# One more pair of feed-forward steps in joined form, in four blocks of a fused RWKV-6 and feed-forward kernel

## The chip, the cores and the metric

The kernel runs on one core of a Trainium2 chip. The metric is the device time of one execution in microseconds (us). All data are float32 in memory; a float32 matmul is issued as two instructions, so counts of matmul instructions in the profile are twice the number of products.

The engines are named as in the profile: PE (TensorE matmuls), PEld (its weight loads), DVE (VectorE), ACT (ScalarE), POOL (GpSimd) and SP (SyncE, which issues most DMAs).

## The reference

```python
batch, n_heads, seq, head_dim = (4, 8, 768, 48)
n_tokens, d_model, d_ff = (3072, 384, 2048)
...
for t in range(S):                       # RWKV-6: a recurrence over the tokens
    kt, vt, rt, wt = (k[:, :, t], v[:, :, t], r[:, :, t], w[:, :, t])
    cur = np.einsum('bhd,bhe->bhde', u[None] * kt, vt)
    y[:, :, t] = np.einsum('bhd,bhde->bhe', rt, state + cur)
    state = wt[:, :, :, None] * state + np.einsum('bhd,bhe->bhde', kt, vt)
...
x = y.transpose(0, 2, 1, 3).reshape(B * S, H * D)
h = x @ w_in
g = h - np.tanh(h)
return (g @ w_out).astype(np.float32)
```

## The kernel before

**Blocks and steps.** The 3072 tokens are worked in 8 blocks of 384 (`NB`), two for each of the 4 sequences. A block's attention output lies in three tiles `xT` of 128 features by 384 tokens. The feed-forward part of a block runs over 16 steps `f`, each for 128 of the 2048 hidden units. The main loop (L1340) runs over the blocks `i` and in each over the steps; `now` is 16 i + f. While the steps of block i run, the attention of block i+1 (`later`) is prepared between them: its operations are put by `plan(i)` (L1145) to certain steps, and DMAs for i+1 and i+2 (`after`) too. For blocks 3 to 6 the plan puts `times_behind` to steps 0 and 1 and `times_before` and `held` to step 3 (all on DVE), the score product `earlier` (PE, the method `gram`, L497) to step 4, the splits, DMA transposes and joins that turn the keys to steps 3 to 9 (the turned keys are collected in the tile `ks`), `update` (PE, L578, the first reader of v) to step 10 and `results` (PE, L772, then ACT copies into `xT` and `late`) to step 12.

**A single step.** `first` (L884) makes h of 128 hidden units by 384 tokens with 3 products (6 instructions, L886) into the PSUM tile `hp`, and ACT scales it (L891). `slight` (L966) then makes g: on ACT the square s of h (L978), a second square qa (L979) and a check (`over`, L983), on DVE two products (L894), the second of which writes g. DVE's two products are not issued with their step but in the next one, as `rest`.

**The second matrix product.** For two steps together (a pair q = f // 2), `form_g` (L1012) makes sums and differences of the six 128x128 pieces of g on DVE, and `Fewer` (L1077) multiplies them with forms of `w_out` in 15 products instead of 18. Six of them are issued by `add` at step 2q+3 and six at step 2q+4; the list `due` holds what is to come, and `add_due` issues it. With the last pair of a block, `add` also evicts the PSUM banks by ACT (`scaled`, L1103); this falls to steps 1 and 2 of the next block. Three products for each pair, the side products, come later (`others`, in part in steps 0 and 1 of the next block, into one of the two PSUM tiles `att`), and `others_summed` (L1118, DVE) reads them.

**A joined pair.** `Twos` (L897) makes h of two steps at once. `weight_forms` (L917) makes five combinations s1 to s5 of the pieces of `w_in`, `token_forms` (L926) four combinations t1 to t4 of the halves of `xT[0]` and `xT[1]`, each 192 tokens wide. `begin` (L934) then issues 11 products of 192 columns (22 instructions, L950) instead of 6 of 384, into both tiles `att`; ACT copies one of the sums (L951), and four DVE additions (L960) give h of both steps, held in the tiles `pre` and `w`. In the kernel before, the pairs 0 to 6 of block 7 and the pair 7 of block 6 (`BEFORE`) are joined; there, no attention work of a next block needs those tiles any more. All forms of `w_in` are made in block 6.

**The order.** PE, DVE, ACT and SP are scheduled by hand (`tc.manual_schedule`): each engine carries its instructions out in the order in which the code issues them. In each step the order is: `first` or `begin`, `slight`'s ACT part, the DVE list `ops`, the phases of the next block, the loads, and what is due. The list `ops` is put together from `rest` (the products of the step before), `formed` and `forming` (forms of g; the second stem from two steps before), `carried`, `behind`, and `spare` (the next block's DVE work); `between` takes two lists in turn. In the even step of a joined pair, `add_due` is called before `slight`. A load may be held back behind the step's scaling instruction, `made` (L1497).

Of the kernel before, what the change touches and what calls it, by code (L numbers as in the profile page):

```python
# [37 lines left out]
F32 = mybir.dt.float32  # L38
# [27 lines left out]
DM = H * D  # L66
FF = 2048
KC = DM // P
NF = FF // P
N = B * S  # L70
BANK = 512
HB = NB // 2
# [46 lines left out]
        ("add", (0, 4, 0), (11, 2, 11)), ("sub", (14, 14, 1)))  # L119
PLACES = ((8, 10, 0), (2, 5, 13), (11, 7, 14))  # L120
TWOS = range(7)
BEFORE = NF // 2 - 1


SLIGHT = 2.0 ** -6
# [4 lines left out]
def kernel(  # L130
# [144 lines left out]
    class Kept:  # L275
# [3 lines left out]
        def __init__(self, pool):  # L279
            self.both, self.n = [pool.tile([P, 2, BANK], F32, name=f"att{j}", tag=f"att{j}") for j in range(2)], 0  # L280
# [42 lines left out]
    class Block:  # L323
# [86 lines left out]

        def begin(self):
            self.xT = [xpool.tile([P, NB], F32, name=f"xT{i}", tag=f"xT{i}") for i in range(KC)]
            self.late = inp.tile([P, NB], F32, name="late", tag="late")
            return self.xT

        def before(self, p0, n):
# [318 lines left out]
        def result_out(self, pairs, copy=None):  # L735

            copies = []
            for p in reversed(pairs):
                n = p // 2
# [153 lines left out]
    def product(out, in0, scalar, in1, op0):  # L893
        return lambda: nc.vector.scalar_tensor_tensor(out=out, in0=in0, scalar=scalar, in1=in1,  # L894
                                                      op0=op0, op1=ALU.mult)

    class Twos:  # L897

        def __init__(self):
            def spare(name):
                return inp.tile([P, 2 * HALF], F32, name=name, tag=name)

            n = NF // 2 * P
            k, r, post = spare("k"), spare("r"), spare("post")
            self.forms = [t[:, 0:n].rearrange("p (j c) -> p j c", c=P) for t in (k, r, post)]
            self.turned = [t[:, n + a * HB:n + (a + 1) * HB] for t in (k, r) for a in range(2)]
            self.to = None

        def more(self):
            n = NF // 2 * P
            ks = work.tile([P, NPAIR * NCP * P], F32, name="ks", tag="ks", bufs=1)
            v_sb = inp.tile([P, NCP * DM], F32, name="v_sb", tag="v_sb")
            self.forms += [t[:, 0:n].rearrange("p (j c) -> p j c", c=P) for t in (ks, v_sb)]

        def weight_forms(self, late):  # L917

            at = w_in_sb.rearrange("p (j two) k c -> p j two k c", two=2)
            (a11, a12, a13), (a21, a22, a23) = ([at[:, :, i, k] for k in range(KC)] for i in range(2))  # L920
            s1, s2, s3, s4, s5 = self.forms if late else self.forms + [None] * 2
            return [lambda op=op, of=of: nc.vector.tensor_tensor(out=of[0], in0=of[1], in1=of[2], op=OPS[op])
                    for op, *of in (("add", s1, a21, a22), ("sub", s2, s1, a11), ("sub", s3, a11, a21),
                                    ("sub", s4, a12, s2), ("sub", s5, a13, a23))[2 if late else 0:5 if late else 2]]

        def token_forms(self, xs):  # L926
# [3 lines left out]
            t1, t2, t3, t4 = self.turned  # L930
            return [lambda of=of: nc.vector.tensor_tensor(out=of[0], in0=of[1], in1=of[2], op=ALU.subtract)
                    for of in ((t1, b12, b11), (t3, b22, b12), (t2, b22, t1), (t4, b21, t2))]

        def begin(self, ps, j):  # L934

            if self.to is None:
                self.to = [inp.tile([P, 2 * HALF], F32, name=name, tag=name)[:, 0:8 * HB].rearrange(
                    "p (n t) -> p n t", t=HB) for name in ("pre", "w")]
            h = self.to[j % 2]
            e0, e1 = ps.both[(ps.n + 1) % 2], ps.both[ps.n % 2]  # L940
            (a11, a12, a13), (_, a22, a23) = ([w_in_sb[:, 2 * j + i, k] for k in range(KC)] for i in range(2))
            s1, s2, s3, s4, s5 = (t[:, j] for t in self.forms)
            t1, t2, t3, t4 = self.turned
            (b11, _), (b21, b22), (b31, b32) = self.first, self.second, self.third
            for to, *of in ((e0[:, 1, 0:HB], (a11, b11)), (e0[:, 0, 0:HB], (a12, b21), (a13, b31)),
                            (e0[:, 0, HB:NB], (s2, t2)), (e1[:, 0, 0:HB], (s3, t3)),
                            (e1[:, 0, HB:NB], (s1, t1), (a23, b32)), (e1[:, 1, 0:HB], (s4, b22), (s5, b32)),
                            (e1[:, 1, HB:NB], (a22, t4), (a23, b31))):
                for n, (lhs, rhs) in enumerate(of):
                    nc.tensor.matmul(to, lhsT=lhs, rhs=rhs, start=n == 0, stop=n + 1 == len(of))  # L950
# [9 lines left out]
            return [lambda of=of: nc.vector.tensor_tensor(out=of[0], in0=of[1], in1=of[2], op=ALU.add)  # L960
                    for of in ((h[:, 0:5:4], twice(h[:, 7]), both(e0[:, 0, 0:NB])),
                               (h[:, 5:7], twice(h[:, 4]), both(e1[:, 0, 0:NB])),
                               (h[:, 1], h[:, 6], e1[:, 1, 0:HB]),
                               (h[:, 2:4], twice(h[:, 5]), e1[:, 1::-1, HB:NB]))]
# [180 lines left out]
    def plan(i):  # L1145
# [15 lines left out]
        else:  # L1161
# [178 lines left out]
    for i, blk in enumerate(blocks):  # L1340
# [9 lines left out]
        for f in range(NF):  # L1350
# [19 lines left out]
            if not joined:  # L1370
                g, ahead_of_h, square, later_ops = slight(h, now, i, f)
            elif f % 2:
                g, ahead_of_h, square, later_ops = slight(twos.h[1], now, i, f, 1.0 / UPSCALE, over)
                for op in over:
                    op()
            else:
                ahead_of_h, square = [], []
# [8 lines left out]
                              if of and not name.startswith("bound")]  # L1386
            if i:
                spare += [lambda n=n: form_w(n, 4 if f < 12 else 6, 2) for n in formed_w.get(f, ())]
            if i == blocks_n - 2:
                if f == 10:  # L1390
                    twos = Twos()
                    spare += twos.weight_forms(False)
                elif f == 13:
                    twos.more()
# [202 lines left out]
```

## Time and profile before

| | |
|---|---|
| time, median of 3 runs | 543.28 us (542.43 to 544.0) |
| profiled execution | 543.27 us, span 541.4 us |
| mean granted TensorE clock | 0.995 of full speed |
| PE busy | 531.2 us (98%) |
| DVE busy | 481.2 us (89%) |
| ACT busy | 396.7 us (73%) |
| block 3, steps 0 to 15 | 216.56 to 280.45 us of the span |
| block 6, steps 0 to 15 | 408.31 to 471.8 us of the span |

The span runs from the first to the last instruction; the time around it is not in the rows. In the rows of a timeline the first number is the start in us from the span's start, the second the length of the group in us, then the engine, the line, the operation, the tiles out<-in, the shape and the count; in brackets stands the engine's idle time before it and what ended it. Matmuls are pipelined, so the length of a group ends later than the next one starts; the distance between two starts is what a group costs. In the rows of groups by shape the numbers behind the bar are busy time in us and the mean of one in ns.

### The profile page before, as it was taken

The numbers are of one execution on the slowest core, as the hardware profiler recorded it, in microseconds if no ns is written. First come the engines' busy times: TensorE is split into PE (matmuls) and PEld (weight loads), VectorE is DVE, ScalarE is ACT, GpSimd is POOL, SyncE is SP. The second block draws the span as 40 slices with busy tenths as digits, with TensorE's granted clock in tenths as the row PEclk, the third lists the DMA queues.
The fourth block names the chain that finished last, engine by engine and source line by source line (L and its number), as shares of the span: only waits on it lengthen the run. The fifth ranks groups of instructions, "written<-read, shape, count | busy, mean of one in ns | idle before, by whom it ended". The sixth has DMA issues, their size and how long they took to land.

```text
span 541.4 us, 15092 instructions
## 1 busy us (share of the span) xinstructions
PE 531.2 (98%) x5780; PEld 415.0 (77%) x5780; DVE 481.2 (89%) x992; ACT 396.7 (73%) x800; POOL 9.3 (2%) x57
## 2 busy tenths in 40 slices
PE   7899999999999999999999999999999999999996
PEld 5756666677887778777877787777877777899994
DVE  7899999999989989799897889979897899979985
ACT  5899996888668876688676887588865986546461
POOL 1100000000000000000000000000000000000001
PEclk9899999999999999999999999999999999999999
DMA  7698632261402632154212532137222320100011
GB/s 276 230 404 333 240 101 96 90 144 60 123 18 80 159 108 69 45 129 138 61 56 61 131 120 65 51 90 161 62 89 68 78 72 17 42 1 0 12 35 47
DMA packets 53048, 56.35 MB, mean 104 GB/s; under 512 B 21488, under 2 KB 50928, under 8 KB 52976
## 3 DMA queue, kind: packets, MB, share of 16 engines
q1 hardware_dynamic: 52592, 55.18, 33.9%
q8 instruction: 49, 0.80, 0.6%
q14 instruction: 23, 0.19, 0.1%
q10 hardware_dynamic: 288, 0.10, 0.1%
q0 software_dynamic: 96, 0.07, 0.1%
HBM read 44.73 MB, written 4.72 MB: 91 GB/s over the span
## 4 chain that ended last, share of the span: by engine, by line
PE 94%; DVE 3%; DMA 1%; issue 1%; SPq 0%; DVEq 0%
PE hp L886 39%; PE acc L1091 27%; PE att L1091 6%; PE acc L1042 5%; PE att L950 5%; PE att L772 4%; PE att L497 2%; PE att L578 1%; PE acc L1069 1%; PE att L886 1%; DMA r<-in_rT 1%; PE acc L886 1%; DVE pre L420 1%; PE hp L1091 0%; PE att L682 0%
## 5 line engine op out<-in xcount | busy, mean ns | idle before, releaser
L886 PE MATMUL hp<-xT,w_sb 128*128 128x384 f32 x642 | 225.6, 488 | 0.5 <-DVE w_sb L271 0.5
L886 PEld LDWEIGHTS hp<-xT,w_sb 128*128 128x128 f32 x642 | 114.8, 190 | 61.2 <-issue 0.6
L1091 PE MATMUL acc<-forms,g 128*128 128x128 f32 x972 | 135.7, 276 | 0.0
L1091 PEld LDWEIGHTS acc<-forms,g 128*128 128x128 f32 x972 | 124.2, 192 | 8.8
L1012 DVE TENSOR_TENSOR g<-g 128x256 f32<-128x256 f32 x270 | 106.5, 420 | 6.4 <-PE acc L1091 5.7
L891 ACT ACTIVATE h<-hp 128x384 f32<-128x384 f32 x107 | 52.6, 491 | 77.6 <-PE hp L886 77.5
L894 DVE SCALAR_TENSOR_TENSOR h<-h,s 128x384 f32<-128x384 f32 x112 | 61.7, 551 | 26.1 <-ACT s L978 25.8
L979 ACT ACTIVATE qa<-s,shift 128x384 f32<-128x384 f32 x113 | 69.6, 616 | 3.7
L983 ACT ACTIVATE junk<-s,shift 128x384 bf16<-128x384 f32 x113 | 67.9, 600 | 0.3
L1091 PE MATMUL acc<-w_sb,g 128*128 128x128 f32 x324 | 54.0, 276 | 0.0
L1091 PEld LDWEIGHTS acc<-w_sb,g 128*128 128x128 f32 x324 | 47.3, 192 | 8.7 <-ACT sums L1059 0.3
L894 DVE SCALAR_TENSOR_TENSOR g<-qa,h 128x384 f32<-128x384 f32 x96 | 52.9, 551 | 0.7
L978 ACT ACTIVATE s<-h 128x384 f32<-128x384 f32 x97 | 50.7, 523 | 3.0
L1126 DVE TENSOR_TENSOR sums<-sums 128x256 f32<-128x256 f32 x84 | 33.4, 410 | 1.2 <-ACT sums L1103 1.0
L1042 PE MATMUL acc<-w_sb,sums 128*128 128x384 f32 x96 | 33.7, 487 | 0.0
L1091 PE MATMUL att<-w_sb,g 128*128 128x128 f32 x200 | 33.4, 275 | 0.0
L267 ACT ACTIVATE up<-raw 128x768 f16<-128x768 f32 (+1 forms) x32 | 33.4, 1080 | 0.0
L1091 PEld LDWEIGHTS att<-w_sb,g 128*128 128x128 f32 x200 | 29.0, 192 | 4.2
L1042 PEld LDWEIGHTS acc<-w_sb,sums 128*128 128x128 f32 x96 | 18.0, 190 | 12.3 <-DVE sums L894 0.3
L420 DVE TENSOR_TENSOR_SCAN pre<-w,start 128x780 f32<-128x780 f32 x14 | 25.0, 1783 | 0.8
L432 DVE TENSOR_TENSOR_SCAN post<-w,seed 128x780 f32<-128x780 f32 x14 | 24.9, 1776 | 0.0
L983 ACT ACTIVATION_READ_ACCUMULATOR junk<-s,shift 128x1 f32 x113 | 21.1, 187 | 0.0
(156 smaller groups left out, 653.5 us busy)
## 6 DMA issues: line engine op xcount, KB each, us to landing
raw<-in_weights SPq DMA_DIRECT2D x16, 768.0 KB, 6.6
w<-in_wT SPq DMA_DIRECT2D x7, 780.0 KB, 4.6
k<-in_kT SPq DMA_DIRECT2D x7, 768.0 KB, 4.5
r<-in_rT SPq DMA_DIRECT2D x7, 768.0 KB, 4.6
v_sb<-in_v SPq DMA_DIRECT2D x8, 576.0 KB, 4.0
k<-in_tokens SPq DMA_DIRECT2D x7, 576.0 KB, 4.9
r<-in_tokens SPq DMA_DIRECT2D x7, 576.0 KB, 4.8
out_y<-sums SPq DMA_DIRECT2D x18, 128.0 KB, 1.8
```

Source lines behind the costliest of these rows:

```text
L267: return lambda: nc.scalar.activation(out=to, in_=of, func=AF.Copy, scale=scale, bias=bias)
L420: return nc.vector.tensor_tensor_scan(out=self.tile("pre")[:, cols], data0=self.tile("w")[:, cols], data1=start[:, 0:n * NCH * LP], initia ...
L886: nc.tensor.matmul(hp, lhsT=w_in_sb[:, f, kc, :], rhs=xT[kc], start=(kc == KC - 1), stop=(kc == 0))
L891: return h, nc.scalar.activation(out=h, in_=hp, func=AF.Copy, scale=1.0 / UPSCALE)
L894: return lambda: nc.vector.scalar_tensor_tensor(out=out, in0=in0, scalar=scalar, in1=in1, op0=op0, op1=ALU.mult)
L978: nc.scalar.activation(out=s, in_=h, func=AF.Square, scale=scale)
L979: nc.scalar.activation(out=qa, in_=s, func=AF.Square, bias=shift[:, 4:5])
L983: nc.scalar.activation(out=junk[:, 0:NB], in_=s, func=AF.Relu, bias=shift[:, 5:6], accum_out=excess[:, at:at + 1])
L1012: return lambda: nc.vector.tensor_tensor(out=G[:, to:to + 2], in0=two(G, g_at(q, a0), g_at(q, a1)), in1=two(G, g_at(q, b0), g_at(q, b1)), ...
L1042: nc.tensor.matmul(acc, lhsT=g[:, j * P:(j + 1) * P], rhs=w_out_sb[:, f, :], start=(f == self.first), stop=(f == NF - 1))
L1091: nc.tensor.matmul(to, lhsT=G[:, g_at(q, a), :], rhs=rhs, start=start, stop=stop, skip_group_check=True)
L1126: ops.append(lambda op=op, at=at: nc.vector.tensor_tensor(out=at[0], in0=at[1], in1=at[2], op=OPS[op]))
```

## The change

Pair 1 (steps 2 and 3) of blocks 3 to 6 is joined too. A second object of `Twos`, `beside`, holds the forms for this one pair. It is made anew in each of the four blocks. The weight forms are made in step 0 of the block and lie, with the first two token forms, in the tile of v (`v_sb`), which is idle then; the token forms are made in step 1, the last two in the tile `late`. The h of the pair goes to the tile `ks`. The load of v for the next block moves from step 1 to step 5. In step 3 of these blocks, and in step 15 of block 6, the DVE list is `forming[:1] + rest + formed + spare`, where it was `forming[:1]` and then `rest + formed` and `spare` in turn.

For the last two blocks, the token forms of block 6 (made in step 13) lie in the unused ends of `post` and `ks` instead of those of `k` and `r`. Those of block 7 keep `k` and `r`; they are made in step 14 of block 6 instead of step 15.

```diff
-BEFORE = NF // 2 - 1
+JOINED = {3: (1,), 4: (1,), 5: (1,), 6: (1, NF // 2 - 1), 7: TWOS}
...
+            if i in JOINED:
+                loads = {3: ["tokens k"], 4: ["tokens r"], 5: ["v"], 7: ["w"], 9: ["k"], 11: ["r"]}
...
-            joined = f // 2 in TWOS if not later else i == blocks_n - 2 and f // 2 == BEFORE
+            joined = f // 2 in JOINED.get(i, ())
+            near = later and f < 4
...
-                outs = twos.begin(ps_a, f // 2)
+                by = beside if near else twos
+                outs = by.begin(ps_a, f // 2)
...
+            if later and i in JOINED and f < 2:
+                if not f:
+                    beside, v_left, late_left = (Twos(1, 1), spare_tile("v_sb", NCP * DM), spare_tile("late", NB))
+                    for x in range(5):
+                        beside.form(x, v_left, x * P)
+                    beside.results(spare_tile("ks", NPAIR * NCP * P, work))
+                    spare += beside.weight_forms(0, 2, 1, 4, 3)
+                else:
+                    spare += beside.token_forms(here, beside.halves((v_left, 5 * P), (late_left, 0)))
             if i == blocks_n - 2:
                 if f == 10:
-                    twos = Twos()
-                    spare += twos.weight_forms(False)
+                    twos = Twos(0, NF // 2)
...
+                    spare += twos.weight_forms(0, 1)
                 elif f == 13:
...
-                    spare = twos.token_forms(here) + twos.weight_forms(True) + spare
-                elif f == 15:
-                    spare += twos.token_forms(xT)
+                    spare = (twos.token_forms(here, twos.halves((post_left, left), (ks_left, left))) +
+                             twos.weight_forms(2, 3, 4) + spare)
+                    twos.results(*(spare_tile(name) for name in ("pre", "w")))
+                elif f == 14:
+                    spare += twos.token_forms(xT, twos.halves((k_left, left), (r_left, left)))
...
-            elif joined and (later or f < 2 * LAST):
+            elif joined and later:
+                ops, carried = forming[:1] + rest + formed + spare, forming[1:]
+            elif joined and f < 2 * LAST:
                 ops, carried = forming[:1] + between(rest + formed, spare), forming[1:]
...
-                g, ahead_of_h, square, later_ops = slight(twos.h[0], now, i, f, 1.0 / UPSCALE, over)
+                g, ahead_of_h, square, later_ops = slight(by.h[0], now, i, f, 1.0 / UPSCALE, over)
```

The lines left out pass the tiles to `Twos` from outside (`form`, `halves`, `results`) where it took them itself, and create the tile `late` at its first use.

More of the change, by code (lines that the diff above doesn't have):

```diff
@@ L412, in begin @@
             self.xT = [xpool.tile([P, NB], F32, name=f"xT{i}", tag=f"xT{i}") for i in range(KC)]
-            self.late = inp.tile([P, NB], F32, name="late", tag="late")
+            self.late = None
             return self.xT
@@ L738, in result_out @@
             for p in reversed(pairs):
+                if self.late is None:
+                    self.late = inp.tile([P, NB], F32, name="late", tag="late")
                 n = p // 2
@@ L895, in product, with spare_tile @@
                                                       op0=op0, op1=ALU.mult)
+    def spare_tile(name, width=2 * HALF, pool=inp):
+        return pool.tile([P, width], F32, name=name, tag=name, bufs=1)
     class Twos:
[L901 to L919, printed above, removed]
+        def __init__(self, base, n):
+            self.base, self.n = base, n
+            self.forms, self.to = [None] * 5, []
@@ new lines, in form, with halves, results, weight_forms @@
+        def form(self, x, t, at=0):
+            self.forms[x] = t[:, at:at + self.n * P].rearrange("p (j c) -> p j c", c=P)
+        def halves(self, *tiles):
+            return [t[:, at + a * HB:at + (a + 1) * HB] for t, at in tiles for a in range(2)]
+        def results(self, *tiles):
+            self.to = [t[:, 0:8 * HB].rearrange("p (n t) -> p n t", t=HB) for t in tiles]
+        def weight_forms(self, *which):
+            at = w_in_sb[:, 2 * self.base:2 * (self.base + self.n)]
+            at = at.rearrange("p (j two) k c -> p j two k c", two=2)
@@ L920, in weight_forms @@
             (a11, a12, a13), (a21, a22, a23) = ([at[:, :, i, k] for k in range(KC)] for i in range(2))
-            s1, s2, s3, s4, s5 = self.forms if late else self.forms + [None] * 2
+            s1, s2, s3, s4, s5 = self.forms
+            every = (("add", s1, a21, a22), ("sub", s2, s1, a11), ("sub", s3, a11, a21), ("sub", s4, a12, s2),
+                     ("sub", s5, a13, a23))
             return [lambda op=op, of=of: nc.vector.tensor_tensor(out=of[0], in0=of[1], in1=of[2], op=OPS[op])
-                    for op, *of in (("add", s1, a21, a22), ("sub", s2, s1, a11), ("sub", s3, a11, a21),
-                                    ("sub", s4, a12, s2), ("sub", s5, a13, a23))[2 if late else 0:5 if late else 2]]
@@ L926, in token_forms @@
-        def token_forms(self, xs):
+                    for op, *of in (every[x] for x in which)]
+        def token_forms(self, xs, turned):
             (b11, b12), (b21, b22), self.third = ([x[:, 0:HB], x[:, HB:NB]] for x in xs)
             self.first, self.second = (b11, b12), (b21, b22)
-            t1, t2, t3, t4 = self.turned
+            self.turned = t1, t2, t3, t4 = turned
             return [lambda of=of: nc.vector.tensor_tensor(out=of[0], in0=of[1], in1=of[2], op=ALU.subtract)
@@ L934, in begin @@
         def begin(self, ps, j):
[L936 to L939, printed above, removed]
+            h = self.to[j % len(self.to)]
             e0, e1 = ps.both[(ps.n + 1) % 2], ps.both[ps.n % 2]
             (a11, a12, a13), (_, a22, a23) = ([w_in_sb[:, 2 * j + i, k] for k in range(KC)] for i in range(2))
-            s1, s2, s3, s4, s5 = (t[:, j] for t in self.forms)
+            s1, s2, s3, s4, s5 = (t[:, j - self.base] for t in self.forms)
             t1, t2, t3, t4 = self.turned
@@ L1372 @@
             elif f % 2:
-                g, ahead_of_h, square, later_ops = slight(twos.h[1], now, i, f, 1.0 / UPSCALE, over)
+                g, ahead_of_h, square, later_ops = slight(by.h[1], now, i, f, 1.0 / UPSCALE, over)
                 for op in over:
@@ L1388 @@
                 spare += [lambda n=n: form_w(n, 4 if f < 12 else 6, 2) for n in formed_w.get(f, ())]
+            if later and i in JOINED and f < 2:
[7 more added lines that the diff above has]
+                    spare += beside.token_forms(here, beside.halves((v_left, 5 * P), (late_left, 0)))
             if i == blocks_n - 2:
                 if f == 10:
-                    twos = Twos()
-                    spare += twos.weight_forms(False)
-                elif f == 13:
-                    twos.more()
-                    spare = twos.token_forms(here) + twos.weight_forms(True) + spare
-                elif f == 15:
-                    spare += twos.token_forms(xT)
+                    twos = Twos(0, NF // 2)
+                    left = twos.n * P
+                    k_left, r_left, post_left = (spare_tile(name) for name in ("k", "r", "post"))
+                    for x, t in enumerate((k_left, r_left, post_left)):
+                        twos.form(x, t)
+                    spare += twos.weight_forms(0, 1)
+                elif f == 13:
+                    ks_left = spare_tile("ks", NPAIR * NCP * P, work)
+                    twos.form(3, ks_left)
+                    twos.form(4, spare_tile("v_sb", NCP * DM))
+                    spare = (twos.token_forms(here, twos.halves((post_left, left), (ks_left, left))) +
[3 more added lines that the diff above has]
+                    spare += twos.token_forms(xT, twos.halves((k_left, left), (r_left, left)))
             adding = []
```

## The prediction

> **What bounds the kernel now.** I read the page's busy shares and its chain first, then the busy time per block, then the timeline of each engine around the steps that the change touches.
>
> ```profile
> PE 531.2 (98%) x5780; PEld 415.0 (77%) x5780; DVE 481.2 (89%) x992; ACT 396.7 (73%) x800; POOL 9.3 (2%) x57
> PE 94%; DVE 3%; DMA 1%; issue 1%; SPq 0%; DVEq 0%
> ...
> 216.56:280.45 63.89, 63.89 (x705) 50.30 (x705) 55.42 (x115) 48.01 (x102) 0.32 (x4) 1.00 0.33 88
> ```
>
> The third row is block 3 (columns: length, then busy time of PE, weight loads, DVE, ACT, POOL, then the granted clock). PE is busy for the whole 63.89 us, DVE for 55.42. So PE's queue is the bound, a microsecond of matmul removed is a microsecond won, and work on DVE is free only as long as no PE instruction waits for it. DVE has 8.47 us to spare per block, so the question is not how much DVE work is added but what comes later by it.
>
> This is what PE and DVE do in block 3 from step 2 (the first that the change joins) to step 5:
>
> ```profile
> 225.62 2.10 PE L886 MATMUL hp<-xT,w_sb 128*128 128x384 f32 x6
> 227.56 1.05 PE L1091 MATMUL acc<-forms,g 128*128 128x128 f32 x8
> ...
> 232.17 2.10 PE L886 MATMUL hp<-xT,w_sb 128*128 128x384 f32 x6
> 234.20 1.63 PE L497 MATMUL att<-pre,post 48*64 48x64 f32 x96
> ...
> 220.99 0.43 DVE L1012 TENSOR_TENSOR g<-g 128x256 f32<-128x256 f32 x1 [0.81 <-PE acc L1091]
> 222.80 0.95 DVE L446 TENSOR_TENSOR post<-k,post 128x768 f32<-128x768 f32 x1
> 224.90 0.56 DVE L894 SCALAR_TENSOR_TENSOR h<-h,s 128x384 f32<-128x384 f32 x1 [1.14 <-ACT s L978]
> ...
> 231.12 1.75 DVE L439 TENSOR_TENSOR pre<-r,pre 128x1536 f32<-128x1536 f32 x1
> ```
>
> Two rows carry the forecast. L497 at 234.20 is the score product of the next block ("earlier", step 4); it reads `pre`, which L439 (`times_before`, the last of step 3's work on DVE) writes from 231.12 to 232.87. The margin is 1.33 us. From step 2's first matmul to L497 it is 234.20 − 225.62 = 8.58 us.
>
> **The change part by part.** *The saved matmuls.* A joined pair already runs in block 7; its second pair (steps 2 and 3) has the same order around it as the new pairs will have, with the last products of the block before and their two evictions behind it:
>
> ```profile
> 481.27 1.14 PE L950 MATMUL att<-xT,w_sb 128*128 128x192 f32 x6
> 484.85 1.05 PE L1091 MATMUL acc<-forms,g 128*128 128x128 f32 x8
> 486.19 0.61 PE L1091 MATMUL acc<-w_sb,g 128*128 128x128 f32 x4
> ...
> 486.39 1.09 ACT L1103 ACTIVATE sums<-acc 128x512 f32<-128x512 f32 x2 [3.29 <-PE acc L1091]
> 487.36 0.52 ACT L978 ACTIVATE s<-w 128x384 f32<-128x384 f32 x1
> ...
> 488.58 0.56 DVE L894 SCALAR_TENSOR_TENSOR g<-qa,w 128x384 f32<-128x384 f32 x1
> 489.51 0.55 DVE L894 SCALAR_TENSOR_TENSOR w<-w,s 128x384 f32<-128x384 f32 x1
> ```
>
> The pair costs 484.85 − 481.27 = 3.58 us. Two single steps cost 2 x (227.56 − 225.62) = 3.88. A part of the products (L1091) takes 486.19 − 484.85 = 1.34. With nothing late, the new way from step 2 to L497 would be pair 3.58, product parts 1.34 + 1.34, step 4's matmuls 1.94, and 0.09 before L497 (234.20 − 232.17 − 1.94): 8.29 us. That is 0.29 won per block, 1.16 over blocks 3 to 6.
>
> *The forms.* They need these durations:
>
> ```profile
> L1126 DVE TENSOR_TENSOR sums<-sums 128x128 f32<-128x128 f32 x7 | 2.2, 313 | 0.0
> L931 DVE TENSOR_TENSOR k<-xT 128x192 f32<-128x192 f32 x2 | 0.7, 352 | 0.0
> ```
>
> Five weight forms of 128x128 in step 0 (5 x 0.313 = 1.57 us) and four token forms in step 1 (4 x 0.352 = 1.41). What covers them is DVE's idle time in those steps, 0.81 and 1.14 us. Step 1's last operation ends at 222.80 + 0.95 = 223.75; with both additions, less the 0.81 that is taken up, it is 225.92 by whole durations. The sum of the side products follows, 0.55, to 226.5. PE begins the pair at 225.62 and needs the first token form 0.98 later and the bank that this sum frees 1.30 later, by the pace of the pair (six of its 22 instructions, then eight, at 3.58 / 22 = 0.163 each): 226.60 and 226.92. Both are met, narrowly by this upper reckoning; consecutive DVE operations overlap by up to 0.1 us, so the true margin is larger. Cost 0; without the cover it would be up to 0.5 us a block. The value tile, `late` and `ks` were last read in the block before and cost no wait.
>
> *The moved wait: this is the cost.* In a single step ACT scales h as soon as PE is done. In a joined pair the order on ACT is: copy of the first product, the two evictions of the last products (queued ahead because `add_due` comes before `slight`), then the square s. The evictions wait for PE to finish the pair and the product part after it. So, counted from the pair's first matmul, s starts at 487.36 − 481.27 = 6.09, the second product g at 488.58 − 481.27 = 7.31, and behind g and its form (L1012) DVE's next instruction at 489.51 − 481.27 = 8.24. The diff puts step 3's other work behind just these (`forming[:1] + rest + formed + spare`), and the spare work there is `times_before`. It will start at 8.24 and end at 8.24 + 1.75 = 9.99. L497 is the next that waits, PE's queue stands behind it, and PE was ready at 8.29. A released PE starts 0.05 after DVE (row 472.81 below), so at 10.04: PE idles 1.75 us in each of four blocks, and each block is 10.04 − 8.58 = 1.46 longer. 4 x 1.46 = 5.84 us. Bounds: between the pair's other instance in block 7, whose s does not stand behind evictions, and this one with another 0.3 of small delays:
>
> ```profile
> 465.56 1.14 PE L950 MATMUL att<-xT,w_sb 128*128 128x192 f32 x6
> 466.53 0.49 PE L950 MATMUL att<-k,r 128*128 128x192 f32 x2
> 470.31 0.52 ACT L978 ACTIVATE s<-w 128x384 f32<-128x384 f32 x1 [2.93 <-DVE w L960]
> ...
> 471.81 1.14 PE L950 MATMUL att<-xT,w_sb 128*128 128x192 f32 x6
> 473.21 0.59 PE L950 MATMUL att<-k,r 128*128 128x192 f32 x2 [0.26 <-DVE k L931]
> 472.81 0.35 DVE L931 TENSOR_TENSOR k<-xT,k 128x192 f32<-128x192 f32 x1
> ```
>
> There s starts 4.75 after the pair, 1.34 earlier, which would leave 0.12 per block. I take 1.46, since the order of block 7's second pair is the one that the code gives.
>
> *Behind the wait.* From there DVE is further behind PE than before, and has its 8.47 us of slack to catch up; the next products that need its forms come more than a step (1.94 + 1.34 = 3.28 us) later. I take 0, up to 0.3 a block. The load of v leaves step 1 and stands on SP's queue behind the r tokens and both transposes of steps 4 and 5:
>
> ```profile
> v_sb<-in_v SPq DMA_DIRECT2D x8, 576.0 KB, 4.0
> ```
>
> It lands in 4.0 us, and v is first read in step 10, five steps or 16.4 us later. Cost 0. The first transpose writes the `ks` tile that now holds the joined values; it waits anyway for ACT's split of step 4, which stands behind the last read of them. The k tokens go out earlier, since the instruction that held them back is now step 1's.
>
> *The separate memory.* In block 7 the first pair waits for a token form that could not be written while the pair before was read: 473.21 − 471.81 = 1.40 against 466.53 − 465.56 = 0.97. The 0.43 goes away: −0.43.
>
> *The clock.* PE's new idle gaps have a neighbour in the trace:
>
> ```profile
> 9.34 1.08 PE L497 MATMUL att<-r,k 48*64 48x64 f32 x48 [0.83 <-ACT k L457]
> 20.91 0.65 PE L497 MATMUL att<-pre,post 48*64 48x64 f32 x18 [1.39 <-issue]
> 9.00:10.00 1.00, 0.66 (x32) 0.60 (x36) 1.00 (x2) 0.79 (x2) 0.00 (x0) 1.00 1.05 379
> 21.00:21.50 0.50, 0.50 (x24) 0.50 (x26) 0.00 (x0) 0.50 (x2) 0.00 (x0) 0.62 0.59 147
> 24.50:25.00 0.50, 0.50 (x19) 0.42 (x12) 0.05 (x1) 0.49 (x2) 0.00 (x0) 0.97 0.91 356
> ```
>
> The gap of 0.83 us left the granted clock at 1.00. The gap of 1.39 was followed by a clock of 0.50 from about 21.2 to 24.5, some 3.4 us, which costs a PE-bound stretch 1.7 us. My gaps are 1.75 us, longer, but they stand between full-size matmuls, while that one stood among small ones. So 0 to 4 drops of 1.7 us, 0 to 6.8. I take one drop, 1.7, nearer to none, because the neighbours differ.
>
> The Trainium skill's page "TensorE: Matmul & The Clock Gate" (Part 1) says that the clock halves after at least one idle window of about 3.4 us, and advises against PE gaps beyond about 3 us; by it, gaps of 1.75 us cost nothing more. The trace agrees in the length of the drop and not in the gap that brings it on.
>
> **Sum.** The profiled execution took 543.27 us (span 541.4); the median is 543.28, so nothing is to be corrected. 543.27 + 5.84 − 0.43 = 548.7 without a drop, and + 1.7 = 550.4.
>
> **Rivals.** (1) The wait as above, the clock never drops: 548.7. For it: the blocks' PE is at work all around the gap. Chance 0.35. (By its page on the clock gate, the Trainium skill expects this case.) (2) Three or four drops: 553.8 to 555.5. For it: the 1.39 us gap; chance 0.20. (3) The other side: `times_before` is finished by the time PE reaches L497. Then only the 0.29 x 4 and 0.43 count: 543.27 − 1.16 − 0.43 = 541.7, a gain. It decides at 8.29 us after the pair's start; break-even is at 8.58, 1.46 earlier than I find. Against it: even with s at 4.75 the wait remains. Chance 0.06, and 0.03 for something between that lands within the limit of measurement.
>
> **How the numbers follow.** The likeliest case, with 0.91, is the wait at L497 in four blocks; its own range runs from 547.5 (1.2 less: shorter waits) to 555.5. One or two drops, which hold the forecast, have 0.36 of it. The range of 547.0 to 555.0 leaves out rival 3, what lies between, and four drops: under 0.2. A measurement of this kernel tells 0.3%, 1.6 us, from no change. Faster 0.06, same 0.03, slower 0.91.
>
> **What would show it.** In blocks 3 to 6: a 22-instruction L950 group of 3.6 us at step 2; L439 starting about 8.2 us behind its start, after the form of g; PE idle some 1.75 us in front of L497, released by DVE; the granted clock at 0.50 behind some of these gaps or not. In block 7: no gap in the first pair. The forecast is wrong if L439 stands ahead of the joined products on DVE, or if s does not stand behind the two L1103 evictions on ACT.

## The result and the profile after

The changed kernel took 549.08 us (median of 6 runs, 547.39 to 551.89), the kernel before 543.64 beside it (6 runs, 541.91 to 544.71). The ratio is 1.0126, with an interval of 1.0106 to 1.0146: slower, by 1.3%. The profiled execution took 548.93 us with a span of 547.2, 5.8 more than before.

In the changed kernel's code the lines of the feed-forward part stand a little lower than before: L886 is now L888, L891 is L893, L894 is L896, L950 and L951 are L951 and L952, L960 is L961, L978 is L979, L1012 is L1013, L1091 is L1092, L1103 is L1104. L439 and L497 are where they were.

Of the page of the changed kernel the busy times and the chain, and from its view of waits the row of L497 (total us, number of waits, longest):

```profile
PE 531.5 (97%) x5820; PEld 421.3 (77%) x5820; DVE 496.7 (91%) x1044; ACT 393.6 (72%) x796; POOL 9.3 (2%) x57
PE 92%; DVE 4%; ACT 2%; DMA 1%; issue 0%; SPq 0%; PEldq 0%; PEld 0%; DVEq 0%
...
PE att L497 <- DVE pre L439: 6.5, 4, 1.6
```

DVE did 15.5 us more and still has 9% to spare. But four waits of PE, which before had none of this kind, make 6.5 us, and DVE's share of the chain rose from 3 to 4%.

The busy times block by block say where the time lies. First the kernel before, blocks 4, 5 and 6 (block 3 is in the prediction), then the changed kernel, blocks 3 to 6:

```profile
280.45:344.42 63.97, 63.97 (x706) 50.37 (x705) 55.55 (x116) 47.99 (x102) 0.32 (x4) 1.00 0.34 93
344.42:408.31 63.89, 63.89 (x705) 50.30 (x705) 55.37 (x115) 47.99 (x102) 0.32 (x4) 1.00 0.35 91
408.31:471.80 63.49, 63.49 (x714) 51.48 (x714) 56.41 (x119) 44.23 (x94) 0.18 (x2) 1.00 0.21 54
```

```profile
215.33:280.69 65.36, 63.73 (x715) 51.65 (x715) 59.11 (x128) 47.24 (x101) 0.32 (x4) 1.00 0.32 87
280.69:347.76 67.07, 65.44 (x715) 53.19 (x715) 59.38 (x129) 47.25 (x101) 0.32 (x4) 0.97 0.32 85
347.76:413.12 65.36, 63.73 (x715) 51.64 (x715) 59.40 (x128) 47.24 (x101) 0.32 (x4) 1.00 0.33 90
413.12:478.25 65.13, 63.50 (x725) 53.01 (x725) 60.40 (x133) 43.62 (x94) 0.18 (x2) 1.00 0.21 54
```

Blocks 3 and 5 are 65.36 − 63.89 = 1.47 longer. Block 4 is 67.07 − 63.97 = 3.10 longer: the same 1.47 and 1.63 more, in a block whose granted clock is 0.97 instead of 1.00. Up to the first matmul of block 7 (478.09 and 471.81 in the timelines) block 6 is 478.09 − 413.12 − (471.81 − 408.31) = 1.47 longer. From there to the end the changed kernel is shorter by (541.4 − 471.81) − (547.2 − 478.09) = 0.48. The beginning, up to block 3, is shorter by 216.56 − 215.33 = 1.23, which has nothing to do with the change (below). The sum is −1.23 + 4 x 1.47 + 1.63 − 0.48 = 5.80, the difference of the spans.

The timeline of the changed kernel in block 3, from step 2 to the score product, PE first, then ACT, then DVE:

```profile
224.39 1.14 PE L951 MATMUL att<-xT,w_sb 128*128 128x192 f32 x6
227.97 1.05 PE L1092 MATMUL acc<-forms,g 128*128 128x128 f32 x8
...
234.44 1.63 PE L497 MATMUL att<-pre,post 48*64 48x64 f32 x96 [1.63 <-DVE pre L439]
...
229.51 1.08 ACT L1104 ACTIVATE sums<-acc 128x512 f32<-128x512 f32 x2 [3.29 <-PE acc L1092]
230.48 0.52 ACT L979 ACTIVATE s<-ks 128x384 f32<-128x384 f32 x1
...
231.70 0.56 DVE L896 SCALAR_TENSOR_TENSOR g<-qa,ks 128x384 f32<-128x384 f32 x1
232.29 0.42 DVE L1013 TENSOR_TENSOR g<-g 128x256 f32<-128x256 f32 x1
232.63 1.75 DVE L439 TENSOR_TENSOR pre<-r,pre 128x1536 f32<-128x1536 f32 x1
```

The pair takes 227.97 − 224.39 = 3.58. The square s stands behind the two evictions on ACT, g behind s on DVE, and `times_before` (L439) behind g and its form. PE's score product starts 10.05 after the pair, and PE has been idle for 1.63 ahead of it.

### The profile page after: what moved, and what is told of

It reads as the page before. It is cut to its first block, busy times and chain, and to the rows that moved or that the text cites. A ratio compares the mean times of both kernels' runs of the same rounds, so it can differ in the third digit from the quotient of the medians.

```text
span 547.2 us, 15161 instructions
## 1 busy us (share of the span) xinstructions
PE 531.5 (97%) x5820; PEld 421.3 (77%) x5820; DVE 496.7 (91%) x1044; ACT 393.6 (72%) x796; POOL 9.3 (2%) x57
## 4 chain that ended last, share of the span: by engine, by line
PE 92%; DVE 4%; ACT 2%; DMA 1%; issue 0%; SPq 0%; PEldq 0%; PEld 0%; DVEq 0%
PE hp L888 34%; PE acc L1092 26%; PE att L951 8%; PE att L1092 6%; PE acc L1043 5%; PE att L774 4%; PE att L497 2%; DVE pre L439 1%; PE att L578 1%; PE acc L1070 1%; PE att L888 1%; DMA r<-in_rT 1%; ACT sums L1104 1%; PE acc L888 1%; DVE pre L420 1%; PE hp L1092 0%
## 5 line engine op out<-in xcount | busy, mean ns | idle before, releaser
L888 PE MATMUL hp<-xT,w_sb 128*128 128x384 f32 x594 | 209.1, 488 | 0.5 <-DVE w_sb L271 0.5
L888 PEld LDWEIGHTS hp<-xT,w_sb 128*128 128x128 f32 x594 | 106.6, 191 | 57.2 <-issue 0.9
L1092 PE MATMUL acc<-forms,g 128*128 128x128 f32 x972 | 137.1, 278 | 0.0
L1092 PEld LDWEIGHTS acc<-forms,g 128*128 128x128 f32 x972 | 125.4, 193 | 7.7
L1013 DVE TENSOR_TENSOR g<-g 128x256 f32<-128x256 f32 x270 | 106.8, 420 | 0.7 <-PE acc L1092 0.2
L893 ACT ACTIVATE h<-hp 128x384 f32<-128x384 f32 x99 | 48.6, 491 | 72.6 <-PE hp L888 72.6
L896 DVE SCALAR_TENSOR_TENSOR h<-h,s 128x384 f32<-128x384 f32 x104 | 57.3, 551 | 13.1 <-ACT s L979 13.0
L1092 PE MATMUL acc<-w_sb,g 128*128 128x128 f32 x324 | 54.3, 277 | 0.0
L1092 PEld LDWEIGHTS acc<-w_sb,g 128*128 128x128 f32 x324 | 47.2, 192 | 7.6 <-ACT sums L1060 0.3
L896 DVE SCALAR_TENSOR_TENSOR g<-qa,h 128x384 f32<-128x384 f32 x88 | 48.5, 551 | 1.3
L979 ACT ACTIVATE s<-h 128x384 f32<-128x384 f32 x89 | 46.6, 524 | 2.8
L1092 PE MATMUL att<-w_sb,g 128*128 128x128 f32 x200 | 33.4, 275 | 0.0
L1092 PEld LDWEIGHTS att<-w_sb,g 128*128 128x128 f32 x200 | 29.0, 192 | 4.2
L951 PE MATMUL att<-xT,w_sb 128*128 128x192 f32 x120 | 25.4, 326 | 0.0
```

The source lines that it names most:

```text
L888: nc.tensor.matmul(hp, lhsT=w_in_sb[:, f, kc, :], rhs=xT[kc], start=(kc == KC - 1), stop=(kc == 0))
L893: return h, nc.scalar.activation(out=h, in_=hp, func=AF.Copy, scale=1.0 / UPSCALE)
L979: nc.scalar.activation(out=s, in_=h, func=AF.Square, scale=scale)
L1013: return lambda: nc.vector.tensor_tensor(out=G[:, to:to + 2], in0=two(G, g_at(q, a0), g_at(q, a1)), in1=two(G, g_at(q, b0), g_at(q, b1)), ...
L1092: nc.tensor.matmul(to, lhsT=G[:, g_at(q, a), :], rhs=rhs, start=start, stop=stop, skip_group_check=True)
```

## The experiments

Each time is given as a ratio to runs of the kernel before on the same chip, whose medians were 542.05 to 542.14 us. My theory was that the whole loss is the place of `times_before` on DVE (1.46 per block), with now and then a clock drop behind a gap. The rivals were: the added DVE work of the forms, or the moved load of v; ACT's order; the separate memory; and gaps that cost no clock at all.

**`times_before` ahead of the joined products.**

```diff
-                ops, carried = forming[:1] + rest + formed + spare, forming[1:]
+                ops, carried = forming[:1] + spare + rest + formed, forming[1:]
```

> The changed kernel, but in step 3 of blocks 3 to 6 times_before and held stand ahead of the joined pair's products on DVE. Theory (the wait at L497 is the loss): L439 starts some 5.1 us behind the pair's first matmul and ends at 6.9, ahead of the 8.29 at which PE reaches L497; PE does not idle there, each block gains 0.29 us, and with 0.43 at block 7 the time is 1.6 us under the kernel before, about 542.0. Rival (the 5 us of DVE work added per block are the loss): the order changes nothing, about 549.

Measured: 542.76 us, ratio 1.0005 (0.9989 to 1.0021). The loss is gone, but the gain that I expected with it isn't there. From the waits and the timeline of this run, block 3, and its busy times:

```profile
PE hp L888 <- ACT h L893: 1.3, 4, 0.3
...
230.02 1.75 DVE L439 TENSOR_TENSOR pre<-r,pre 128x1536 f32<-128x1536 f32 x1
232.93 1.63 PE L497 MATMUL att<-pre,post 48*64 48x64 f32 x96
...
237.07 2.19 ACT L545 COPY w<-post 128x768 uint16<-128x768 uint16 x2
239.16 0.48 ACT L893 ACTIVATE h<-hp 128x384 f32<-128x384 f32 x1
239.70 2.20 PE L888 MATMUL hp<-xT,w_sb 128*128 128x384 f32 x6 [0.33 <-ACT h L893]
...
215.52:279.77 64.25, 63.92 (x715) 51.73 (x715) 59.10 (x128) 47.14 (x101) 0.32 (x4) 1.00 0.33 90
```

L439 ends 1.16 before L497 starts, so PE no longer waits there. The next that is late is ACT: the two splits (L545, 2.19 us) hold up the scaling of step 5, which frees `hp` for step 6. PE waits 0.33 in each of the four blocks, and block 3 takes 64.25 against 63.89.

**`times_before` between the joined products**, as in the kernel before:

```diff
+                ops, carried = forming[:1] + between(rest + formed, spare), forming[1:]
```

> The changed kernel, but in step 3 the DVE list takes the products and times_before in turn, as the kernel before had it for joined steps. Theory: L439 starts behind the first product only, at about 7.1 us, ends at 8.87; PE idles 0.6 us at L497, a block is 0.34 longer than before, 4 x 0.34 - 0.43 = 0.9 over the kernel before, about 544.5, and the clock does not drop behind gaps this short. Rival (added DVE work): about 549.

Measured: 543.72 us, ratio 1.0019 (1.0007 to 1.0032), 1.0 us more than before; expected was 0.9. The row of the waits shows the same gap, cut to a third:

```profile
PE att L497 <- DVE pre L439: 2.0, 4, 0.5
```

**The separate memory alone**: pair 1 of blocks 3 to 6 is worked in single steps, no forms are made for it, and v is loaded in step 1 as before:

```diff
-JOINED = {3: (1,), 4: (1,), 5: (1,), 6: (1, NF // 2 - 1), 7: TWOS}
+JOINED = {6: (NF // 2 - 1,), 7: TWOS}
+FORMED = ()
...
-            if i in JOINED:
+            if i in FORMED:
...
-            if later and i in JOINED and f < 2:
+            if later and i in FORMED and f < 2:
```

> Only the second part of the change: separate memory for the token forms of the last two blocks, no new joined pair, v loaded in step 1 as before. Theory: 0.43 us less than the kernel before (543.2), within the limit of measurement. Rival (the moved forms in steps 13 to 15 cost something): slower than before.

Measured: 541.86 us, ratio 0.9996 (0.9984 to 1.0009). By time a gain of 0.43 (0.0008) can be told neither from none nor from twice as much. The trace has the answer; these are the rows of block 7's first pair in the changed kernel, which keeps this part:

```profile
478.09 1.14 PE L951 MATMUL att<-xT,w_sb 128*128 128x192 f32 x6
479.07 0.49 PE L951 MATMUL att<-k,r 128*128 128x192 f32 x2
```

The distance is 0.98, where it was 1.40 before: 0.42 less.

**The forms without their use.** The five and four forms are made in steps 0 and 1 and v is loaded in step 5, but the pair is worked in single steps:

```diff
-JOINED = {3: (1,), 4: (1,), 5: (1,), 6: (1, NF // 2 - 1), 7: TWOS}
+JOINED = {6: (NF // 2 - 1,), 7: TWOS}
+FORMED = (3, 4, 5, 6)
...
-            if i in JOINED:
+            if i in FORMED:
...
-            if later and i in JOINED and f < 2:
+            if later and i in FORMED and f < 2:
...
-                    beside.results(spare_tile("ks", NPAIR * NCP * P, work))
```

> The forms of pair 1 are made in steps 0 and 1 of blocks 3 to 6 and v is loaded in step 5, as in the changed kernel, but steps 2 and 3 stay single and the forms are not used. Theory: DVE's idle time covers the 3.0 us of forms per block and the later load of v costs nothing: as e3, 543.2. Rival (added DVE work, or the moved load): a part of the loss shows here, 3/5 of it would be 3 us, about 546.5.

Measured: 541.67 us, ratio 0.9983 (0.9972 to 0.9995). The added DVE work and the moved load cost nothing that shows. That rival falls.

**The squares ahead of the evictions on ACT** (pair 1 of blocks 3 to 6):

```diff
-                add_due(now)
+                if not near:
+                    add_due(now)
                 over = []
                 g, ahead_of_h, square, later_ops = slight(by.h[0], now, i, f, 1.0 / UPSCALE, over)
+                add_due(now)
```

> The changed kernel, but in step 2 of blocks 3 to 6 the square s and qa of the pair's first half are issued on ACT ahead of the two evictions. Theory (times_before stands behind a chain that starts with s, and s behind the evictions): s starts at 4.75 us behind the pair's first matmul instead of 6.09, L439 at 6.9 instead of 8.24, and PE idles about 0.4 us at L497 instead of 1.6. A first experiment showed a second wait that comes next, PE's step 6 for ACT's scaling of step 5 (0.33 us by its trace); with ACT's work only reordered, most of it stays. So 4 x (0.07 + 0.3) - 0.43, about 1 us over the kernel before. Rival (evictions do not matter, s waits for DVE's additions): as the changed kernel, 5.5 us over.

Measured: 544.68 us, ratio 1.0045 (1.0031 to 1.006): 2.4 us more than before, where I expected about 1. From its waits and its timeline in block 3:

```profile
PE acc L1092 <- ACT sums L1104: 2.0, 4, 0.5
...
225.86 1.14 PE L951 MATMUL att<-xT,w_sb 128*128 128x192 f32 x6
230.61 0.52 ACT L979 ACTIVATE s<-ks 128x384 f32<-128x384 f32 x1 [2.93 <-DVE ks L961]
231.69 1.06 ACT L1104 ACTIVATE sums<-acc 128x512 f32<-128x512 f32 x2
232.32 0.71 PE L1092 MATMUL acc<-forms,g 128*128 128x128 f32 x4 [0.49 <-ACT sums L1104]
232.89 1.75 DVE L439 TENSOR_TENSOR pre<-r,pre 128x1536 f32<-128x1536 f32 x1
234.90 1.63 PE L497 MATMUL att<-pre,post 48*64 48x64 f32 x96
```

The square starts 4.75 after the pair (225.86), as in block 7's first pair, and L439 at 232.89 − 225.86 = 7.03 instead of 8.24. But now the evictions are late, and PE waits 0.49 for the banks that they free. Step 2's pair follows the one of the block before after 64.36, against 63.89: 0.47 per block, 1.9 over four blocks, less 0.48 in block 7, so 1.4. The profile has a span of 543.1, 1.7 more than before's, both with a clock drop in the start. The rest, up to 2.4, fits the clock of the timed executions: five of this kernel's six have a mean granted clock of 0.995 to 0.997, of the kernel before only three of 17. The sixth, at 0.999, took 543.47, which is 1.4 above the 542.05 of the kernel before.

**The gap filled.** Ahead of L497 in these blocks PE gets, by the argument `ahead` of `gram` (which the kernel so far uses in its start), five matmuls of 128x512 in bf16 that nobody uses:

```diff
-                return [getattr(self, name)(ps, p0) for p0 in HALVES]
+                filled = name == "earlier" and self.b * NQ + self.q > 3
+                return [getattr(self, name)(ps, p0, ahead=5 if filled and p0 == HALVES[0] else 0) for p0 in HALVES]
```

> The changed kernel, with five bf16 matmuls of 128x512 without use put on PE ahead of L497 in blocks 3 to 6, so that PE works through most of the 1.6 us in which it waits for times_before. L497 starts no earlier. Theory (some executions also lose 1.7 us per clock drop that the idle gap brings on): the clock stays at 1.00 behind L497 in every block, and the time is 4 x 1.47 - 0.43 = 5.45 us over the kernel before in nearly all executions, with less spread than the changed kernel's 547.4 to 551.9. Rival (the drops come from something else): the same spread and drops as the changed kernel, 5.5 to 8 us over.

Measured: 547.5 us, ratio 1.0104 (1.0088 to 1.012). Row of the waits and timeline of block 3:

```profile
PE att L497 <- DVE pre L439: 2.2, 4, 0.6
...
232.20 1.24 PE L308 MATMUL att<-ident 128*128 128x512 bf16 x5
234.00 1.63 PE L497 MATMUL att<-pre,post 48*64 48x64 f32 x96 [0.56 <-DVE pre L439]
```

PE's idle time goes from 6.5 to 2.2 us and the loss stays: it is DVE's lateness, not PE's idleness. The granted clock is 1.00 throughout blocks 3 to 6 of this run.

**The gap doubled.** One more DVE operation of the same size (the maximum of r with itself) ahead of `times_before`:

```diff
-                ops, carried = forming[:1] + rest + formed + spare, forming[1:]
+                twice = []
+                if f == 3:
+                    r = later.tokens("r")
+                    twice = [lambda r=r: nc.vector.tensor_tensor(out=r, in0=r, in1=r, op=ALU.max)]
+                ops, carried = forming[:1] + rest + formed + twice + spare, forming[1:]
```

> The changed kernel, with one more DVE operation of 128x1536 (a maximum of the r tile with itself, which leaves it as it is) ahead of times_before in blocks 3 to 6. Theory (what DVE does ahead of times_before in step 3 goes to the time in full): 4 x 1.67 = 6.7 us more than the changed kernel, and PE's gap at L497 grows to 3.3 us. If a gap of some 1.4 us within a window of the clock gate is enough for a drop, each of the four brings one: 5.45 + 6.7 + 6.8, about 19 us over the kernel before. If the clock drops only behind a longer gap, 12.2 over. Rival (PE's wait is not set by DVE's queue): no change against the changed kernel.

Measured: 563.47 us, ratio 1.0382 (1.0361 to 1.0403): 0.0382 x 542.05 = 20.7 us more than before. The waits, the score product of block 3, and windows behind the gaps of blocks 3 and 6 (the clock is the third number from the end):

```profile
PE att L497 <- DVE pre L439: 13.7, 4, 3.4
...
237.10 1.63 PE L497 MATMUL att<-pre,post 48*64 48x64 f32 x96 [3.43 <-DVE pre L439]
...
238.50:242.00 3.50, 3.50 (x30) 3.13 (x23) 3.50 (x11) 1.43 (x2) 0.00 (x0) 0.53 0.76 89
...
444.00:447.00 3.00, 3.00 (x87) 2.88 (x81) 2.51 (x7) 2.22 (x4) 0.00 (x0) 0.50 0.35 66
447.00:450.00 3.00, 3.00 (x12) 2.50 (x12) 2.55 (x6) 0.00 (x0) 0.00 (x0) 0.50 1.22 165
```

Behind every gap of 3.43 us (those of blocks 4 and 5 too) the clock falls to 0.50, once for twice as long. Five drops of 1.7 us are 8.5; four gaps longer by 3.43 − 1.63 = 1.80 than in the changed kernel make 4 x (1.47 + 1.80) − 0.48 = 12.6. Together 21.1, so here the gaps drop the clock each time.

**The pair joined in block 3 alone.**

```diff
-JOINED = {3: (1,), 4: (1,), 5: (1,), 6: (1, NF // 2 - 1), 7: TWOS}
+JOINED = {3: (1,), 6: (NF // 2 - 1,), 7: TWOS}
+FORMED = (3,)
...
-            if i in JOINED:
+            if i in FORMED:
...
-            if later and i in JOINED and f < 2:
+            if later and i in FORMED and f < 2:
```

The forms and the later load of v are left in block 3 alone too.

> Pair 1 is joined in block 3 alone, in the way of the changed kernel (and the separate memory of the last two blocks). Theory (each joined pair costs its own block 1.47 us by the wait at L497, and nothing carries over from block to block): 1.47 - 0.43 = 1.0 us over the kernel before, 1.7 more in the executions in which its one gap brings a clock drop. Rival (a cost that exists once, however many blocks are joined): 5 us or none.

Measured: 543.03 us, ratio 1.0021 (1.0002 to 1.0039): 1.1 us, expected 1.0. So the loss is one per block. Its profiled execution, one of its longer ones (546.06), had a clock drop behind the one gap, beside one in the start (from 22.98). By the added line of code, L497 and L439 are L498 and L440 here:

```profile
236.07 1.63 PE L498 MATMUL att<-pre,post 48*64 48x64 f32 x96 [1.64 <-DVE pre L440]
...
238.00:241.00 3.00, 3.00 (x14) 2.69 (x13) 3.00 (x10) 2.69 (x4) 0.00 (x0) 0.50 0.17 34
```

**The splits earlier too.** Beside the first experiment's order, two of ACT's three splits move from steps 3 and 4 to step 1, so that only one is left ahead of the scaling of step 5:

```diff
+                phases.update({1: ("split 2 0", "split 2 1"), 3: (), 4: ("earlier", "turned 2", "split 0 01")})
-                ops, carried = forming[:1] + rest + formed + spare, forming[1:]
+                ops, carried = forming[:1] + spare + rest + formed, forming[1:]
```

> The kernel of e1 (times_before ahead of the joined products), and two of ACT's splits of the keys for the next block issued in step 1 instead of steps 3 and 4, where ACT stands idle for 3.3 us during the pair. Theory (with the wait at L497 gone, ACT is the next to be late, and PE's step 6 waits for its scaling of step 5, 0.5 us a block): ACT reaches step 5 about 1.6 us earlier, this wait goes, and the pair's 0.29 us per block and 0.43 at block 7 are left: 1.6 us under the kernel before, ratio 0.997. Rival (e1 stayed level with the kernel before for another reason): as e1, ratio 1.000.

Measured: 541.48 us, ratio 0.9984 (0.9973 to 0.9996). This is the only version with joined pairs in blocks 3 to 6 that is faster than the kernel before, by 0.9 us, where 1.6 was expected. From its timeline, block 3, and its busy times in blocks 3 to 5:

```profile
225.49 1.14 PE L951 MATMUL att<-xT,w_sb 128*128 128x192 f32 x6
225.87 1.55 ACT L545 COPY w<-post 128x768 uint16<-128x768 uint16 x2
233.83 1.63 PE L497 MATMUL att<-pre,post 48*64 48x64 f32 x96
238.97 0.49 ACT L893 ACTIVATE h<-hp 128x384 f32<-128x384 f32 x1 [0.28 <-PE hp L888]
...
216.42:280.08 63.66, 63.66 (x715) 51.66 (x715) 59.04 (x128) 47.12 (x101) 0.32 (x4) 1.00 0.34 91
280.08:343.80 63.72, 63.72 (x715) 51.71 (x715) 59.09 (x129) 47.08 (x101) 0.32 (x4) 1.00 0.34 90
343.80:407.46 63.66, 63.66 (x716) 51.65 (x715) 59.23 (x128) 47.10 (x101) 0.32 (x4) 1.00 0.36 92
```

Neither wait is left: ACT has waited 0.28 for PE when the scaling of step 5 starts, and a block takes 0.23 to 0.25 less than before. The span is 539.6 against 541.4, both with a clock drop in the start. The kernel whose forms are unused has nearly the same ratio, 0.9983, so the two ratios alone don't show that joining wins. Sorted by clock they differ: over the executions with a mean granted clock of 0.998 or more, the median of this kernel (four executions) is 1.4 below that of the kernel before, and that of the kernel with unused forms (ten) 0.35 below. The blocks of the trace and block 7 give 4 x 0.24 + 0.48 = 1.4 too. This sorting was made after the runs, and four executions are few.

**The changed kernel again**, beside the last two:

> The changed kernel once more, beside the kernel before on this chip. Theory: four waits of 1.47 us less 0.43, 5.45 us over the kernel before where no clock drop falls in, and 1.7 more for each that does: executions between 5 and 10 us over, ratio 1.010 to 1.015, above the 1.0104 of the kernel whose gap is filled. Rival (the executions of the first measurement with a lower clock were chance): 1.0100 as with the filled gap, and the same spread.

Measured: 548.74 us, ratio 1.0116 (1.0097 to 1.0135), again with one clock drop in blocks 3 to 6 of its profile, in block 4. The interval holds the 1.0104 of the kernel with the filled gap, so the times can't tell what the drops add; only the traces show them.

## Why the prediction was right

*The moved wait: right, to a tenth.* Counted from the pair's first matmul in block 3:

| | forecast | measured |
|---|---|---|
| s on ACT | 6.09 | 230.48 − 224.39 = 6.09 |
| g on DVE | 7.31 | 231.70 − 224.39 = 7.31 |
| L439 starts | 8.24 | 232.63 − 224.39 = 8.24 |
| L497 starts | 10.04 | 234.44 − 224.39 = 10.05 |
| loss per block | 1.46 | 1.47 |

PE's idle time is 1.63 and not 1.75, because the group ahead of it counts as busy until its last modelled end; the distance between the starts is what I forecast. That the order on DVE is the cause is shown by the first two experiments: nothing but the place of the spare work of step 3 (`times_before` and, behind it, `held`) was changed, and the wait went to none and to 0.5.

*The forms and the load of v: 0, right*, shown by the run in which they are made and not used. *Behind the wait: 0, right* (1.47 against 1.46 leaves no room). *The separate memory:* −0.43 forecast, −0.48 in the trace; not resolved by time.

*The saved matmuls: the size was a little high.* Where no wait is left, a block gains 0.23 to 0.25, not 0.29: from the pair to L497 it took 8.34 and not 8.29.

*The clock: one drop taken, one found in the profiled execution.* That the two agree is luck: the forecast only bounded how many come, between 0 and 4, and chose one. The executions differ: of the first six, two had a mean granted clock of 1.000, one of 0.997, two of 0.994 and one of 0.989, with times from 547.39 to 551.89 in that order. The median, 549.08, lies nearer to the sum without a drop (548.7) than to the forecast of 550.4.

*The base of the sum was too high.* I took the profiled 543.27 as it was, "so nothing is to be corrected". In its start it held a gap of 1.39 us and a clock drop behind it, whose rows I quoted without asking whether each execution has them. The changed kernel's profile has neither, and its beginning is 1.23 shorter. The change isn't the reason: the kernels with the squares ahead and with the splits earlier have the changed kernel's code up to block 3, and their profiles do have the drop. Of the 35 executions of the kernel before that stand beside the first experiments, 26 have a mean granted clock of 0.998 or more, with a median of 541.99; the profiled one had 0.995. With the measured terms the sum is 543.27 − 1.23 + 5.88 − 0.48 + 1.63 = 549.07 (the profiled execution took 548.93); the forecast lies 1.3 above it, nearly all of it the 1.23 that I left in the base.

*What was still missing after the result* was the next engine: the first experiment's expectation held only DVE's order to be late. With that repaired ACT is late, and most of the gain expected there came only with a second change, the earlier splits.

## What to carry to other kernels

An operation that moves behind others on an in-order engine is priced by the start of the last one ahead of it, counted from a common event, against the start of its first reader; here this gave the loss per block to 0.01 us, where totals of busy time (9% of DVE idle) would have said that nothing happens. When one wait is repaired, look for the next late engine before counting the gain: here the gain appeared only once ACT's queue was put in order too. Before a profiled time becomes the base of a sum, take out of it what other executions of the same kernel needn't have, such as a clock drop.

## What the runs showed of the hardware

A short PE gap can halve the clock, but doesn't each time. The timeline of the changed kernel in block 4 and windows behind the gap (granted clock third from the end):

```profile
299.80 1.63 PE L497 MATMUL att<-pre,post 48*64 48x64 f32 x96 [1.63 <-DVE pre L439]
...
301.20:301.40 0.20, 0.20 (x17) 0.13 (x9) 0.20 (x2) 0.20 (x1) 0.00 (x0) 1.00 0.00 0
301.40:301.60 0.20, 0.20 (x5) 0.20 (x2) 0.20 (x2) 0.20 (x1) 0.00 (x0) 0.58 0.00 0
304.60:304.80 0.20, 0.20 (x2) 0.12 (x1) 0.20 (x2) 0.00 (x0) 0.00 (x0) 0.50 1.15 221
304.80:305.00 0.20, 0.20 (x2) 0.16 (x1) 0.20 (x1) 0.00 (x0) 0.00 (x0) 0.89 1.16 211
```

Means of 0.58 and 0.89 put the drop from 301.43 to 304.84: 3.41 us, which costs 1.7. The same gap in blocks 3, 5 and 6 brought none. The kernel before had a drop in its start (from 21.12) and one at its end:

```profile
539.80:540.00 0.20, 0.00 (x0) 0.00 (x0) 0.00 (x0) 0.00 (x0) 0.00 (x0) 0.86 0.00 0
540.00:540.20 0.20, 0.00 (x0) 0.00 (x0) 0.00 (x0) 0.00 (x0) 0.00 (x0) 0.50 0.00 0
```

It begins at 539.94, so 518.82 us, 152.0 times 3.413, behind the first. The drops behind the doubled gaps begin 68.27 us, 20.0 times 3.413, apart (238.73, 306.99, 375.26 and 443.53). That fits a clock that is decided at the end of fixed windows of 3.41 us. On this grid block 4's gap (298.17 to 299.80) lies whole in the window from 298.02 to 301.43. In block 3 the gap is split into 0.36 and 1.27 by the boundary at 233.17, in block 5 into 1.05 and 0.59, in block 6 into 0.54 and 1.09.

So the position seems to matter, but the idle time that falls in one window doesn't decide alone. The other traces have more cases, each on the grid of its own drops. In the changed kernel's second trace, for example, the drop in block 4 begins at 301.13, so a window begins 20 windows earlier, at 232.86. Block 3's gap of 1.64 us ends at 234.25; the window holds its last 1.39 us, and the clock stays at 1.00.

| part of a gap that lies in one window | us | drop at the window's end |
|---|---|---|
| changed kernel, block 4 | 1.63 | yes |
| changed kernel again, block 4 | 1.64 | yes |
| joined in block 3 alone, block 3 | 1.46 | yes |
| changed kernel again, block 3 | 1.39 | no |
| gap doubled, block 3, the gap's first part | 1.64 | no |
| kernel before, start | 1.39 | yes |
| joined in block 3 alone, start | 1.11 | yes |

The gaps of the start stand among small matmuls. In the first four rows the score product (matmuls of 48x64) follows in the same window; in the fifth the window holds only the larger matmuls of the feed-forward part ahead of the gap. That small matmuls count less than large ones as work would fit all seven rows (the limit would lie between 1.39 and 1.46 us ahead of a score product), but no run tests it, and none sets a gap's position.

The Trainium skill's page "TensorE: Matmul & The Clock Gate" (Part 1) names such windows of about 3.4 us, and the length agrees. It wants at least one whole idle window before the clock halves. In its section "Why this matters for your kernels" it warns of gaps beyond about 3 us. The gaps of 3.43 us dropped the clock each time; but gaps of 1.63 and 1.64 us did so too, in one block of four here and in the run with one joined block.
